# Attention and channel mix in one hand-ordered slot pipeline, heads in pairs, LayerNorm scale at the final add

## Chip, core and metric

The kernel runs on one core of one Trainium2 chip. The metric is the device time of one execution in microseconds (us), the median of several runs; lower is better. Below, PE is the matrix engine (TensorE; its weight loads are PEld), DVE the vector engine, ACT the scalar engine, POOL the GpSimd engine and SP the engine that only issues DMAs.

## What is computed

The reference is a decayed linear attention followed by a channel mix with LayerNorm and a residual. B, H, S, D are 4, 8, 768, 48; the model width is C = 384 and the hidden width F = 1536.

```python
def _attn_ref(r, k, v, w, u):
    for t in range(S):
        kt, vt, rt = (k[:, :, t].copy(), v[:, :, t].copy(), r[:, :, t].copy())
        cur = np.einsum('bhd,bhe->bhde', u[None] * kt, vt)
        y[:, :, t] = np.einsum('bhd,bhde->bhe', rt, state + cur)
        state = w[None, :, :, None] * state + np.einsum('bhd,bhe->bhde', kt, vt)
...
def _moe_ref(x, g_ln, w_ch1, w_ch2):
    xn = (x - mu) / np.sqrt(var + 1e-06) * g_ln
    ch = np.maximum(xn @ w_ch1, 0.0) @ w_ch2
    return (x + ch).astype(np.float32)
```

All inputs and the output are float32; the kernel computes its products in bf16 and sums them in float32.

## The kernel before

Time is cut into 24 tiles of 128 tokens (4 batches of 6). The kernel has two stages, and the instruction order on each engine inside a stage is chosen by the framework's scheduler from the dependencies; nothing is ordered by hand.

Set-up (lines 96 to 208): a table of powers of the decay is built on DVE by doubling (`_powers2`, lines 19 to 52), transposed on PE (lines 144 and 152) and copied into `F2`, the factors by which r and k are scaled.

Attention (lines 287 to 418), for each tile: POOL issues three DMAs that convert r, k and v to bf16 (lines 295, 299, 303; r and k have 4 buffers). DVE scales r and k (`sc`, line 308) and forms the current-token term (`uk`, `rk`, `cc8`, `Vb`, lines 312 to 318). Then, for two groups of four heads each: eight transposes per group (lines 331 and 337), one head at a time, a copy to `trb` on ACT (line 344), four score products (`at_ps`, line 348), a copy on ACT and a mask multiply on DVE (`Bm`, lines 356 and 357), and products of 48 columns for the output and the state (lines 372, 380, 388, 396). The state is scaled on DVE (`zr`, line 404). The attention result `x_sb` (line 411) stays on chip for all 24 tiles.

Channel mix (lines 428 to 467): only after the attention has given its PSUM banks back. The tiles go in six groups of four. LayerNorm statistics and the normalised `xn` come from DVE and ACT (lines 240 to 253), three transposes per tile from PE (line 267), each copied on ACT with the LayerNorm gain (line 270). `hps` (line 441) multiplies by w1 with 512 columns at a time, the ReLU goes to DVE and ACT in turn (lines 449 and 451), `ops` (line 456) multiplies by w2 with 384 columns, and DVE adds the residual (`ot`, line 464) before SP stores it (line 467). The two weights are loaded by POOL with a cast (lines 220 and 221).

Of the kernel before, what the change touches and what calls it, by code (L numbers as in the profile page):

```python
# [12 lines left out]
AX = mybir.AxisListType  # L13

MM_DT = BF16
AT_DT = BF16


def _powers2(nc, tilefn, seed_w, D, H, ncols1, ncols2):
    PW = tilefn([D, H, ncols1], FP32, name="PW2")  # L20
    PI = tilefn([D, H, ncols2], FP32, name="PI2")
    nc.vector.memset(PW[:, :, 0:1], 1.0)
    nc.vector.memset(PI[:, :, 0:1], 1.0)
    seed_w(PW[:, :, 1])
    nc.vector.reciprocal(out=PI[:, :, 1:2], in_=PW[:, :, 1:2])
    n1 = 2
    n2 = 2
    while n1 < ncols1 or n2 < ncols2:
        for T, n, ncols in ((PW, n1, ncols1), (PI, n2, ncols2)):
            if n >= ncols:  # L30
                continue
            nc.vector.tensor_tensor(
                out=T[:, :, n : n + 1],
                in0=T[:, :, n - 1 : n],
                in1=T[:, :, 1:2],
                op=ALU.mult,
            )
        for T, n, ncols in ((PW, n1, ncols1), (PI, n2, ncols2)):
            if n >= ncols:
                continue  # L40
            hi = min(2 * n, ncols)
            cnt = hi - (n + 1)
            if cnt > 0:
                nc.vector.tensor_tensor(
                    out=T[:, :, n + 1 : hi],
                    in0=T[:, :, 1 : 1 + cnt],
                    in1=T[:, :, n : n + 1].to_broadcast([D, H, cnt]),
                    op=ALU.mult,
                )
        n1 = min(2 * n1, ncols1)  # L50
        n2 = min(2 * n2, ncols2)
    return PW, PI
# [3 lines left out]
def kernel(  # L56
# [23 lines left out]
    NTT = B * NCH  # L80
    TG = 4
    NG = NTT // TG

    assert D <= DP
    assert H % 2 == 0 and S % L == 0
    assert C % P == 0 and F % P == 0
    assert NTT % TG == 0
# [33 lines left out]
    if AT_DT == FP32:  # L121
        mask_at = mask_f
    else:
        mask_at = const.tile([P, P], AT_DT, name="mask_at")
        nc.vector.tensor_copy(mask_at[:], mask_f[:])

    PW2, PI2 = _powers2(
        nc,
        const.tile,
        lambda col: nc.sync.dma_start(out=col, in_=w.rearrange("h d -> d h")),  # L130
        D,
        H,
        2 * L,
        2 * L + 1,
    )

    PWtokP = const.tile([P, H, DP], AT_DT, name="PWtokP")
    INVtokP = const.tile([P, H, DP], AT_DT, name="INVtokP")
    nc.vector.memset(PWtokP[:, :, D:DP], 0.0)
    nc.vector.memset(INVtokP[:, :, D:DP], 0.0)  # L140
    with tc.tile_pool(name="ps_setup", bufs=1, space=bass.MemoryType.PSUM) as ps_setup:
        pw_ps = ps_setup.tile([P, H, D], FP32, name="pw_ps")
        for hh in range(H):
            nc.tensor.transpose(
                out=pw_ps[:, hh, :],
                in_=PW2[:, hh, L : 2 * L],
                identity=ident_f[:D, :D],
            )
        nc.scalar.copy(out=PWtokP[:, :, :D], in_=pw_ps[:])
        iv_ps = ps_setup.tile([P, H, D], FP32, name="iv_ps")  # L150
        for hh in range(H):
            nc.tensor.transpose(
                out=iv_ps[:, hh, :],
                in_=PI2[:, hh, L + 1 : 2 * L + 1],
                identity=ident_f[:D, :D],
            )
        nc.scalar.copy(out=INVtokP[:, :, :D], in_=iv_ps[:])

    F2 = const.tile([P, 2, H, DP], AT_DT, name="F2")
    nc.vector.tensor_copy(out=F2[:, 0, :, :], in_=PWtokP[:])  # L160
    nc.vector.tensor_copy(out=F2[:, 1, :, :], in_=INVtokP[:])

    WLq = const.tile([D, H, D], FP32, name="WLq")
    nc.vector.tensor_copy(out=WLq[:], in_=PW2[:, :, L : L + 1].to_broadcast([D, H, D]))

    U_f = const.tile([P, H, D], FP32, name="U_f")
    nc.sync.dma_start(
        out=U_f[:],
        in_=bass.AP(tensor=u.tensor, offset=u.offset, ap=[[0, P], *u.ap]),
    )  # L170
    U_b = const.tile([P, H, D], AT_DT, name="U_b")
# [12 lines left out]
    rk_bufs = []
    for i in range(NSTG):
        rkt = const.tile([P, 2, H, DP], AT_DT, name=f"rk_st{i}")
        nc.gpsimd.memset(rkt[:, :, :, D:DP], 0.0)
        rk_bufs.append(rkt)

    HG = 4  # L190
    NHG = H // HG
    assert H % HG == 0
    NTRB = 4
    trb = []
    for i in range(NTRB):
        t_ = const.tile([P, 2 * HG, P], AT_DT, name=f"trb{i}")
        nc.vector.memset(t_[:], 0.0)
        trb.append(t_)
    trb_ctr = [0]

    zr = []
    for g_ in range(NHG):
        group_slots = []
        for i in range(2):
            z_ = const.tile([P, HG, D], AT_DT, name=f"zr{g_}_{i}")
            nc.vector.memset(z_[:], 0.0)
            group_slots.append(z_)
        zr.append(group_slots)
# [289 lines left out]
```

## Time and profile before

| | us |
|---|---|
| median of 3 runs | 233.95 |
| lowest, highest run | 232.15, 234.10 |
| span of the profiled execution, first to last instruction | 232.1 |
| PE busy, DVE busy, ACT busy, POOL busy in the span | 188.6, 163.9, 121.3, 67.0 |

The profile describes one execution. Its span leaves out what lies around the first and the last instruction; no time of that execution beyond its span is given, and the runs lie between 0.05 and 2.0 us above the span. Busy times are unions of the recorded instructions of an engine. Matrix products are pipelined, so a record of a product is longer than the distance to the next one, and PE's cost is read from that distance. "Granted clock" is the share of full TensorE clock that the chip allowed: 1.00 is 2.4 GHz and 0.50 is 1.2 GHz, a value between them is a mixture of the two over a stretch.

### The profile page before, as it was taken

The page shows a single profiled execution, that of the slowest core. Times are in us where ns is not written, and L with a number is a line of the kernel's source. Part 1 is how long each engine was busy: PE and PEld are TensorE (multiplying, and loading weights), DVE is VectorE, ACT ScalarE, POOL GpSimd, SP SyncE. Part 2 cuts the span into 40 slices and gives each one's busy share as a digit, 9 for nine tenths or more (in the row PEclk, how much of TensorE's full clock was granted, in tenths as well). Part 3 has the DMA queues.
Part 4 walks back from the last instruction along what each step waited for, and adds up shares of the span by engine and source line. Part 5 has one row for each costly group of instructions (what it writes and reads, how often), then busy time and mean ns, then how long its engine had stood idle before and what let it go on. Part 6 is the DMA issues. An engine that isn't in the chain of part 4 may idle for free.

```text
span 232.1 us, 4707 instructions
## 1 busy us (share of the span) xinstructions
PE 188.6 (81%) x1799; PEld 119.2 (51%) x1808; DVE 163.9 (71%) x437; ACT 121.3 (52%) x232; POOL 67.0 (29%) x86
## 2 busy tenths in 40 slices
PE   0059657959778778696767999999999999999993
PEld 0048546748556556475543445445455455455451
DVE  4998798796998999989998895742733534343431
ACT  2018955667668697766768851831732722621310
POOL 9955644656556676741000000000000000000000
PEclk9999875695998999979955899999999999999999
DMA  5999999799999999993000002102002002002012
GB/s 53 109 127 186 123 188 103 40 72 66 58 82 86 65 78 80 69 89 17 3 1 3 0 0 103 37 0 102 34 3 102 34 30 101 7 34 103 3 55 80
DMA packets 81255, 14.66 MB, mean 63 GB/s; under 512 B 76113, under 2 KB 80849, under 8 KB 81233
## 3 DMA queue, kind: packets, MB, share of 16 engines
q0 software_dynamic: 76832, 9.44, 66.8%
q1 hardware_dynamic: 4400, 4.92, 6.2%
q8 instruction: 14, 0.23, 0.4%
q14 instruction: 9, 0.07, 0.1%
HBM read 19.07 MB, written 4.72 MB: 103 GB/s over the span
## 4 chain that ended last, share of the span: by engine, by line
PE 60%; DVE 18%; ACT 8%; issue 7%; DMA 4%; POOL 1%; SPq 0%; ACTq 0%; POOLq 0%; DVEq 0%
PE ops L456 20%; PE hps L441 20%; PE tr_ps L331 5%; PE at_ps L348 4%; PE tr_ps L337 4%; ACT trb L344 4%; DVE sc L308 3%; PE tp L267 3%; DVE x_sb L411 2%; DVE Vb L318 2%; ACT xnT_all L270 2%; DMA rk_st<-in_r_dram 2%; DVE Bm L357 1%; ACT Bm L356 1%; DMA U_f<-in_u_dram 1%
## 5 line engine op out<-in xcount | busy, mean ns | idle before, releaser
L344 ACT COPY trb<-tr_ps 48x1024 bf16<-48x1024 bf16 x48 | 46.6, 1004 | 26.7 <-PE tr_ps L337 26.6
L441 PE MATMUL hps<-xnT_all,w_sb 128*128 128x512 bf16 x207 | 56.6, 388 | 0.5 <-DVE hT L449 0.2
L456 PE MATMUL ops<-w_sb,hT 128*128 128x384 bf16 x288 | 51.8, 326 | 0.0
L449 DVE TENSOR_SCALAR hT<-hps 128x512 bf16<-128x512 f32 x36 | 24.8, 689 | 21.9 <-PE hps L441 21.5
L456 PEld LDWEIGHTS <-hT 128*128 128x128 bf16 x288 | 27.6, 98 | 22.3 <-ACT hT L451 1.5
L270 ACT ACTIVATE xnT_all<-tp,g_sb 128x128 bf16<-128x128 bf16 x72 | 23.3, 368 | 26.8 <-PE tp L267 26.1
L451 ACT ACTIVATE hT<-hps 128x512 bf16<-128x512 f32 x36 | 21.5, 597 | 28.6 <-PE hps L441 28.5
L441 PEld LDWEIGHTS <-w_sb 128*128 128x128 bf16 x216 | 20.7, 99 | 25.4 <-issue 8.1
L464 DVE TENSOR_TENSOR ot<-ops,x_sb 128x384 f32<-128x384 f32 x24 | 13.4, 557 | 28.3 <-PE ops L456 28.3
L356 ACT CAST Bm<-at_ps 128x512 bf16<-128x512 f32 x48 | 28.0, 583 | 5.2 <-PE at_ps L348 4.6
L331 PE MATMUL tr_ps<-ident_mm,sc 128*48 128x128 bf16 x192 | 23.9, 251 | 5.9 <-DVE sc L308 5.9
L348 PE MATMUL at_ps<-trb 128*128 128x128 bf16 x192 | 22.4, 250 | 7.5 <-ACT trb L344 6.9
L303 POOL DMA_DIRECT2D v_st<-in_v_dram x24 | 21.3, 889 | 22.1 <-PE y_all L380 15.1
L372 PE MATMUL y_all<-v_st,Bm 128*128 128x48 bf16 x192 | 16.9, 192 | 11.3 <-DVE Bm L357 11.2
L295 POOL DMA_DIRECT2D rk_st<-in_r_dram x24 | 21.5, 895 | 9.6 <-DVE rk L314 4.6
L337 PE MATMUL tr_ps<-ident_mm,sc 128*48 128x128 bf16 x192 | 24.2, 251 | 0.0
L357 DVE TENSOR_TENSOR Bm<-Bm,mask_at 128x512 bf16<-128x512 bf16 x48 | 19.7, 419 | 5.5 <-ACT Bm L356 4.4
L299 POOL DMA_DIRECT2D rk_st<-in_k_dram x24 | 21.3, 890 | 6.7 <-DVE uk L312 4.1
L372 PEld LDWEIGHTS <-Bm 128*128 128x128 bf16 x192 | 11.8, 99 | 16.8 <-DVE Bm L357 14.8
L348 PEld LDWEIGHTS <-trb 128*128 128x128 bf16 x192 | 12.8, 109 | 13.3 <-ACT trb L344 11.6
L331 PEld LDWEIGHTS <-sc 128*48 128x48 bf16 x192 | 14.0, 116 | 9.5 <-DVE sc L308 7.5
L267 PE MATMUL tp<-ident_mm,xn 128*128 128x128 bf16 x72 | 15.8, 233 | 2.4 <-ACT xnT_all L270 1.4
(57 smaller groups left out, 245.7 us busy)
## 6 DMA issues: line engine op xcount, KB each, us to landing
out_dram<-ot SPq DMA_DIRECT2D x24, 192.0 KB, 1.9
rk_st<-in_r_dram POOLq DMA_DIRECT2D x24, 96.0 KB, 3.9
rk_st<-in_k_dram POOLq DMA_DIRECT2D x24, 96.0 KB, 4.0
v_st<-in_v_dram POOLq DMA_DIRECT2D x24, 96.0 KB, 3.7
w_sb<-in_moe_w_ch_dram POOLq DMA_DIRECT2D x2, 1152.0 KB, 9.9
U_f<-in_u_dram SPq DMA_DIRECT2D x1, 192.0 KB, 3.1
PW<-in_w_dram SPq DMA_DIRECT2D x1, 1.5 KB, 2.1
g_sb<-in_moe_g_ln_dram SPq DMA_DIRECT2D x1, 1.5 KB, 2.8
```

Of the source, the lines that this page charges most:

```text
L267: nc.tensor.transpose(out=tp[:], in_=xn[:, kc * P : (kc + 1) * P], identity=ident_mm[:])
L270: nc.scalar.activation(out=xnT_all[:, kc, tt_ln * P : (tt_ln + 1) * P], in_=tp[:], func=ACT.Copy, scale=g_sb[:, kc : kc + 1],)
L331: nc.tensor.transpose(out=tr_ps[:, hl, :], in_=rsc[:, h0 + hl, :D], identity=ident_at[:],)
L337: nc.tensor.transpose(out=tr_ps[:, HG + hl, :], in_=ksc[:, h0 + hl, :D], identity=ident_at[:],)
L344: nc.scalar.copy(out=tr_sb[:D, :, :], in_=tr_ps[:])
L348: nc.tensor.matmul(out=at_ps[:, hl, :], lhsT=tr_sb[:, HG + hl, :], rhs=tr_sb[:, hl, :], start=True, stop=True,)
L356: nc.scalar.copy(out=Bm[:], in_=at_ps[:])
L357: nc.vector.tensor_tensor(out=Bm[:], in0=Bm[:], in1=mask_at[:].unsqueeze(1).to_broadcast([P, HG, P]), op=ALU.mult,)
L372: nc.tensor.matmul(out=y_all[:, hh, :], lhsT=Bm[:, hl, :], rhs=vs[:, hh, :], start=True, stop=(c == 0),)
L441: nc.tensor.matmul(out=hps[:], lhsT=w1_sb[:, kc, fk * P : (fk + 1) * P], rhs=xnT[:, kc, :], start=(kc == 0), stop=(kc == CK - 1),)
L449: nc.vector.tensor_relu(hT[:, fk, :], hps[:])
L456: nc.tensor.matmul(out=ops[:], lhsT=hT[:, fk, ti * P : (ti + 1) * P], rhs=w2_sb[:, fk, :], start=(fk == 0), stop=(fk == FK - 1),)
```

## The change

The body of the kernel function is written anew, and `_powers2` is gone; the lines that are removed are those of the listing above. One loop of 29 slots takes the place of the two stages, and the order on all five engines is the order in which the program is written (`manual_schedule`). In slot s the attention of tile s, the first product of the channel mix for half a group (`up`, groups of two tiles, three slots behind) and the second product for tile s-5 (`down`) are issued in alternation. So slots 0 to 2 hold attention alone, 3 and 4 attention and `up`, 5 to 23 all three, 24 to 26 `up` and `down`, and 27 and 28 `down` alone.

Other edits: two heads share one transpose of 128 columns (8 instead of 16 per tile), with one ACT copy for all; the score products read 48 rows that start at partition 0 or 64. The mask multiply reads PSUM directly (no ACT copy). The state of two heads is one 96-column block, and a zero pattern in `WLZ` removes the cross terms. The current-token term is a product with `uwI` on PE, copied by ACT (`cc`) and multiplied with v on POOL (`Vb`). The gain of the LayerNorm is multiplied into w1 once (three ACT instructions on `w1_f`, which SP loads in float32); x minus its mean goes through the products, and the reciprocal deviation is applied with the residual (`ot`). All ReLUs run on ACT. Products of `up` have 256 columns.

Not shown in the diff: the decay table `T` is one tile of 128 partitions for both signs of the exponent, doubled in 7 steps on DVE; `WLZ` and `uwI` are built after it on DVE; SP issues six small loads before those of `w1_f`; `ident` and `mask` are made on POOL after `load(0)`. Flags of products are cut.

```diff
@@ -55,413 +16,404 @@
...
+    ld = ctx.enter_context(tc.tile_pool(name="ld", bufs=8))
+    sb2 = ctx.enter_context(tc.tile_pool(name="sb2", bufs=2))
+    sb3 = ctx.enter_context(tc.tile_pool(name="sb3", bufs=3))
+    sm = ctx.enter_context(tc.tile_pool(name="sm", bufs=4))
+    xp = ctx.enter_context(tc.tile_pool(name="xp", bufs=10))
+    ps_h = ctx.enter_context(tc.tile_pool(name="ps_h", bufs=2, space=bass.MemoryType.PSUM))
+    ps = ctx.enter_context(tc.tile_pool(name="ps", bufs=1, space=bass.MemoryType.PSUM))
+    ctx.enter_context(
+        tc.manual_schedule(
+            engines={ENG.PE, ENG.DVE, ENG.Activation, ENG.Pool, ENG.SP}
+        )
+    )
...
+    def load(i):
+        b, c = divmod(i, NCH)
+        s0 = c * L
+        rk = ld.tile([P, 2, H, D], BF16, name="rk")
+        vv = ld.tile([P, H, D], BF16, name="vv")
+        nc.gpsimd.dma_start(out=rk[:, 1], in_=k[b, :, s0 : s0 + L, :].rearrange("h t d -> t h d"))
+        nc.gpsimd.dma_start(out=rk[:, 0], in_=r[b, :, s0 : s0 + L, :].rearrange("h t d -> t h d"))
+        nc.gpsimd.dma_start(out=vv[:], in_=v[b, :, s0 : s0 + L, :].rearrange("h t d -> t h d"))
+        rk_t[i], v_t[i] = rk, vv
...
+    load(0)
...
+    w1_f = const.tile([P, CK, F], FP32, name="w1_f")
+    w1_src = moe_w_ch1.rearrange("(kc p) f -> p kc f", p=P)
+    for kc in range(CK):
+        nc.sync.dma_start(out=w1_f[:, kc, :], in_=w1_src[:, kc, :])
+    w1_sb = const.tile([P, CK, F], BF16, name="w1_sb")
...
+    load(1)
+    load(2)
...
+    fps = ps.tile([P, 2, 512], FP32, name="at")
+    for kc in range(CK):
+        nc.tensor.transpose(out=fps[:, 0, kc * P : (kc + 1) * P], in_=T[:, kc, 0:L], identity=ident_f[:])
+    for kc in range(CK):
+        nc.tensor.transpose(out=fps[:, 1, kc * P : (kc + 1) * P], in_=T[:, CK + kc, 1 : L + 1], identity=ident_f[:])
+    F2 = const.tile([P, 2, H, D], BF16, name="F2")
+    nc.scalar.copy(out=F2[:], in_=fps[:, :, :C].rearrange("p a (h d) -> p a h d", h=H))
...
+    for kc in range(CK):
+        nc.scalar.activation(
+            out=w1_sb[:, kc, :], in_=w1_f[:, kc, :], func=ACT.Copy, scale=g_sb[:, kc : kc + 1]
+        )
...
+    def scale(i):
+        nc.vector.tensor_tensor(
+            out=sc_bufs[i % NSC][:, :, :, :D], in0=rk_t[i][:], in1=F2[:], op=ALU.mult
+        )
+    def transposes(i):
+        sc = sc_bufs[i % NSC].rearrange("p a (q e) d -> p (a q) (e d)", e=2)
+        tp = ps.tile([P, 2 * HP, P], BF16, name="tr")
+        for j in range(2 * HP):
+            nc.tensor.transpose(out=tp[:, j, :], in_=sc[:, j, :], identity=ident[:])
+        tr = sb3.tile([P, 2, HP, P], BF16, name="trs")
+        nc.scalar.copy(out=tr[:], in_=tp[:].rearrange("p (a q) t -> p a q t", a=2))
+        q = sb2.tile([P, HP, P], BF16, name="q")
+        nc.vector.tensor_tensor(out=q[:], in0=tr[:, 0], in1=tr[:, 1], op=ALU.mult)
+        tr_t[i] = tr
+        st[i] = q
+    def scores(i):
+        b, c = divmod(i, NCH)
+        tr, q = tr_t[i], st[i]
+        at = ps.tile([P, 2, HP, P], FP32, name="at")
+        for p in range(HP):
+            for par in range(2):
+                p0 = par * DP
+                nc.tensor.matmul(
+                    out=at[:, par, p, :],
+                    lhsT=tr[p0 : p0 + D, 1, p, :],
+                    rhs=tr[p0 : p0 + D, 0, p, :],
...
+                )
+        s_ps = ps.tile([P, 512], FP32, name="s")
+        ksc = sc_bufs[i % NSC].rearrange("p a (q e) d -> p a q (e d)", e=2)
+        first = True
+        if c < NCH - 1:
+            if c > 0:
+                nc.tensor.matmul(
+                    out=s_ps[:, : HP * E2],
+                    lhsT=ident[:],
+                    rhs=Z_t[i - 1][:].rearrange("p q e -> p (q e)"),
...
+                )
+                first = False
+            for p in range(HP):
+                nc.tensor.matmul(
+                    out=s_ps[:, p * E2 : (p + 1) * E2],
+                    lhsT=ksc[:, 1, p, :],
+                    rhs=v_t[i][:, 2 * p : 2 * p + 2, :],
...
+                )
+                first = False
+        for p in range(HP):
+            nc.tensor.matmul(
+                out=s_ps[:, C + 2 * p : C + 2 * p + 2],
+                lhsT=q[:, p, :],
+                rhs=uwI[:, p, :],
...
+            )
+            first = False
+        A = sb2.tile([P, 2, HP, P], BF16, name="A")
+        for par in range(2):
+            nc.vector.tensor_tensor(
+                out=A[:, par],
+                in0=at[:, par],
+                in1=mask[:].unsqueeze(1).to_broadcast([P, HP, P]),
+                op=ALU.mult,
+            )
+        cc = sb2.tile([P, H], FP32, name="cc")
+        nc.scalar.copy(out=cc[:], in_=s_ps[:, C : C + H])
+        Vb = sb2.tile([P, H, D], BF16, name="Vb")
+        nc.gpsimd.tensor_tensor(
+            out=Vb[:], in0=v_t[i][:], in1=cc[:].unsqueeze(2).to_broadcast([P, H, D]), op=ALU.mult
+        )
+        if c < NCH - 1:
+            Z = sb3.tile([P, HP, E2], BF16, name="Z")
+            nc.vector.tensor_tensor(
+                out=Z[:],
+                in0=s_ps[:, : HP * E2].rearrange("p (q e) -> p q e", q=HP),
+                in1=WLZ[:],
+                op=ALU.mult,
+            )
+            Z_t[i] = Z
+        A_t[i] = A
+        cc_t[i] = Vb
+    def values(i):
+        b, c = divmod(i, NCH)
+        y = ps.tile([P, 512], FP32, name="y")
+        first = True
+        if c > 0:
+            for p in range(HP):
+                nc.tensor.matmul(
+                    out=y[:, p * E2 : (p + 1) * E2],
+                    lhsT=tr_t[i][:, 0, p, :],
+                    rhs=Z_t[i - 1][:, p, :],
...
+                )
+                first = False
+        for par in range(2):
+            for p in range(HP):
+                h = 2 * p + par
+                nc.tensor.matmul(
+                    out=y[:, h * D : (h + 1) * D],
+                    lhsT=A_t[i][:, par, p, :],
+                    rhs=v_t[i][:, h, :],
...
+                )
+                first = False
+        x = xp.tile([P, C], FP32, name="x")
+        nc.vector.tensor_tensor(
+            out=x[:], in0=y[:, :C], in1=cc_t[i][:].rearrange("p h d -> p (h d)"), op=ALU.add
+        )
+        stats = sm.tile([P, nc.vector.BN_STATS_DIM], FP32, name="stats")
+        nc.vector.bn_stats(out=stats[:], in_=x[:])
+        if i % GT == 0:
+            mv_t[i // GT] = sm.tile([P, GT, nc.vector.BN_AGGR_DIM], FP32, name="mv", bufs=6)
+        mv = mv_t[i // GT]
+        nc.vector.bn_aggr(out=mv[:, i % GT, :], in_=stats[:])
+        xn = sb3.tile([P, C], BF16, name="xn")
+        nc.vector.tensor_scalar(
+            out=xn[:], in0=x[:], scalar1=mv[:, i % GT, 0:1], scalar2=None, op0=ALU.subtract
+        )
+        x_t[i], xn_t[i] = x, xn
+        if i % GT == GT - 1:
+            rs = sm.tile([P, GT], FP32, name="rs", bufs=6)
+            nc.scalar.activation(out=rs[:], in_=mv[:, :, 1], func=ACT.Sqrt, bias=eps_t[:], scale=1.0)
+            nc.vector.reciprocal(out=rs[:], in_=rs[:])
+            mv_t[i // GT] = rs
...
+    def ln_transposes(i):
+        g, j = divmod(i, GT)
+        if j == 0:
+            xT_t[g] = sb3.tile([P, CK, GW], BF16, name="xT")
+        tp = ps.tile([P, 2 * HP, P], BF16, name="tr")
+        for kc in range(CK):
+            nc.tensor.transpose(out=tp[:, kc, :], in_=xn_t[i][:, kc * P : (kc + 1) * P], identity=ident[:])
+        nc.scalar.copy(out=xT_t[g][:, :, j * P : (j + 1) * P], in_=tp[:, :CK, :])
+    def up(g, m):
+        if m == 0:
+            hT_t[g] = sb2.tile([P, FK, GW], BF16, name="hT")
+        hp = ps_h.tile([P, 2, GW], FP32, name="hp")
+        for f in range(2):
+            fk = 2 * m + f
+            for kc in range(CK):
+                nc.tensor.matmul(
+                    out=hp[:, f, :],
+                    lhsT=w1_sb[:, kc, fk * P : (fk + 1) * P],
+                    rhs=xT_t[g][:, kc, :],
...
+                )
+        nc.scalar.activation(out=hT_t[g][:, 2 * m : 2 * m + 2, :], in_=hp[:], func=ACT.Relu)
+    NM = 3
+    PM = FK // NM
+    def down(i, m):
+        g, j = divmod(i, GT)
+        if m == 0:
+            o_t[i] = ps.tile([P, 512], FP32, name="o")
+        o = o_t[i]
+        for fk in range(m * PM, (m + 1) * PM):
+            nc.tensor.matmul(
+                out=o[:, :C],
+                lhsT=hT_t[g][:, fk, j * P : (j + 1) * P],
+                rhs=w2_sb[:, fk, :],
...
+            )
+        if m == NM - 1:
+            ot = sb3.tile([P, C], FP32, name="ot")
+            nc.vector.scalar_tensor_tensor(
+                out=ot[:],
+                in0=o[:, :C],
+                scalar=mv_t[g][:, j : j + 1],
+                in1=x_t[i][:],
+                op0=ALU.mult,
+                op1=ALU.add,
+            )
+            b, c = divmod(i, NCH)
+            nc.sync.dma_start(out=out[b, c * L : (c + 1) * L, :], in_=ot[:])
...
+    UP0 = 3
+    DN0 = 5
+    NB = FK // 2
+    def up_slot(s, n_):
+        q_ = s - UP0
+        if q_ < 0:
             return
+        g, j = divmod(q_, GT)
+        if g < NT // GT:
+            up(g, j * (NB // GT) + n_)
+    def down_slot(s, n_):
+        i_ = s - DN0
+        if 0 <= i_ < NT:
+            down(i_, n_)
+    scale(0)
+    for s in range(NT + DN0):
+        att = s < NT
+        if att:
+            transposes(s)
+        if s + 3 < NT and s + 3 not in rk_t:
+            load(s + 3)
+        if s == 0:
             nc.gpsimd.dma_start(out=w2_sb[:], in_=w2_src)
+        up_slot(s, 0)
+        down_slot(s, 0)
+        if att:
+            scores(s)
+            if s + 1 < NT:
+                scale(s + 1)
+        up_slot(s, 1)
+        if 0 <= s - 1 < NT:
+            ln_transposes(s - 1)
+        down_slot(s, 1)
+        if att:
+            values(s)
+        up_slot(s, 2)
+        down_slot(s, 2)
```

## Rows read from the trace of the kernel before

**Rows 1.** The page's chain of work that ended last, share of the span by engine.

```profile
PE 60%; DVE 18%; ACT 8%; issue 7%; DMA 4%; POOL 1%; SPq 0%; ACTq 0%; POOLq 0%; DVEq 0%
```

**Rows 2.** Windows: stretch and its length, busy us (instructions) per engine, clock, DMA, GB/s.

```profile
30.00:46.00 16.00, 12.07 (x157) 9.56 (x153) 13.53 (x38) 8.66 (x14) 8.75 (x10) 0.65 1.38 106
58.00:70.00 12.00, 9.10 (x156) 7.05 (x153) 11.86 (x31) 7.80 (x11) 7.05 (x9) 0.93 1.30 70
...
137.70:232.10 94.40, 89.91 (x503) 46.87 (x507) 41.56 (x83) 33.07 (x85) 0.00 (x0) 1.00 0.14 51
```

**Rows 3.** Chain in order of time, 150 to 163 us: start, us, work (PE at full clock).

```profile
153.47 1.29 PE hps L441 x6
154.76 6.88 PE ops L456 x42
161.64 0.11 PE tp L267 x2
```

**Rows 4.** Timeline of PE at full clock: start, us; first and last of 8 in alternation.

```profile
82.33 0.19 PE L388 MATMUL s_ps<-v_st,sc 128*48 128x48 bf16 x1
...
82.50 0.18 PE L396 MATMUL s_ps<-zr,ident_mm 128*48 128x48 bf16 x1
```

**Rows 5.** Groups by line, ACT: busy us, mean ns of one | idle before.

```profile
L344 ACT COPY trb<-tr_ps 48x1024 bf16<-48x1024 bf16 x48 | 46.6, 1004 | 26.7 <-PE tr_ps L337 26.6
L451 ACT ACTIVATE hT<-hps 128x512 bf16<-128x512 f32 x36 | 21.5, 597 | 28.6 <-PE hps L441 28.5
L157 ACT CAST INVtokP<-iv_ps 128x384 bf16<-128x384 f32 x1 | 0.5, 478 | 0.9 <-PE iv_ps L152 0.9
L244 ACT ACTIVATE rstd<-mv,eps_t 128x1 f32<-128x1 f32 x24 | 6.6, 291 | 1.6 <-DVE mv L242 1.5
```

**Rows 6.** Groups by line, DVE.

```profile
L449 DVE TENSOR_SCALAR hT<-hps 128x512 bf16<-128x512 f32 x36 | 24.8, 689 | 21.9 <-PE hps L441 21.5 <-PE tp L267 0.5
L357 DVE TENSOR_TENSOR Bm<-Bm,mask_at 128x512 bf16<-128x512 bf16 x48 | 19.7, 419 | 5.5 <-ACT Bm L356 4.4
L308 DVE TENSOR_TENSOR sc<-rk_st,F 128x1024 bf16<-128x1024 bf16 x24 | 16.2, 678 | 0.0
L411 DVE TENSOR_TENSOR x_sb<-y_all,Vb 128x384 f32<-128x384 f32 x24 | 13.2, 552 | 0.9 <-PE y_all L380 0.8
L318 DVE TENSOR_TENSOR Vb<-v_st,cc 128x384 bf16<-128x384 bf16 x24 | 13.1, 544 | 0.0
L240 DVE BATCH_NORM_STATS2 stats<-x_sb 128x6 f32<-128x384 f32 x24 | 12.5, 536 | 0.0
L253 DVE TENSOR_SCALAR xn<-x_sb,mv,rstd 128x384 bf16<-128x384 f32 x24 | 11.7, 487 | 1.4 <-PE tp L267 1.2
L242 DVE BATCH_NORM_AGGREGATE mv<-stats 128x2 f32<-128x6 f32 x24 | 3.6, 165 | 0.0
```

**Rows 7.** Timeline of DVE: two instructions that don't wait for each other.

```profile
118.10 0.52 DVE L240 BATCH_NORM_STATS2 stats<-x_sb 128x6 f32<-128x384 f32 x1
118.55 0.53 DVE L318 TENSOR_TENSOR Vb<-v_st,cc 128x384 bf16<-128x384 bf16 x1
```

**Rows 8.** Groups by line, POOL: a DMA issue and an elementwise instruction.

```profile
L303 POOL DMA_DIRECT2D v_st<-in_v_dram x24 | 21.3, 889 | 22.1 <-PE y_all L380 15.1 <-PE y_all L372 6.0 <-DVE Vb L318 0.9
masks.py:199 POOL TENSOR_SCALAR_AFFINE_SELECT ident_f<-ident_f 128x128 f32<-128x128 f32 x1 | 0.3, 287 | 0.0
```

**Rows 9.** The page's DMA issues: KB each as written, median us from issue to landing.

```profile
rk_st<-in_r_dram POOLq DMA_DIRECT2D x24, 96.0 KB, 3.9
w_sb<-in_moe_w_ch_dram POOLq DMA_DIRECT2D x2, 1152.0 KB, 9.9
```

**Rows 10.** Chain in order of time: end of the power table, first transposes, last instruction.

```profile
11.14 1.13 DVE PI L44
...
16.14 0.62 PE tr_ps L331 x4
...
228.39 0.56 DVE ot L464
```

More of the change, by code (lines that the diff above doesn't have):

```diff
@@ L12 @@
 ACT = mybir.ActivationFunctionType
[L13 to L52, printed above, removed]
+ENG = mybir.EngineType
 @with_exitstack
@@ L79 @@
     FK = F // P
[L80 to L87, printed above, removed]
+    GT = 2
+    GW = GT * P
+    E2 = 2 * D
+    assert D <= DP and H % 2 == 0 and S % L == 0 and C % P == 0 and F % P == 0
     assert tuple(out.shape) == (B, S, C)
     const = ctx.enter_context(tc.tile_pool(name="const", bufs=1))
-    xpool = ctx.enter_context(tc.tile_pool(name="xpool", bufs=1))
-    x_sb = xpool.tile([P, NTT, C], FP32, name="x_sb")
@@ L120 @@
     )
[L121 to L171, printed above, removed]
@@ L184 @@
[L184 to L208, printed above, removed]
@@ L263, in emit_ln_transposes @@
-    def emit_ln_transposes(tt_ln, ps_tp):
-        xn = xn_tiles.pop(tt_ln)
-        for kc in range(CK):
-            tp = ps_tp.tile([P, P], MM_DT, name="tp")
-            nc.tensor.transpose(
-                out=tp[:], in_=xn[:, kc * P : (kc + 1) * P], identity=ident_mm[:]
-            )
-            nc.scalar.activation(
-                out=xnT_all[:, kc, tt_ln * P : (tt_ln + 1) * P],
-                in_=tp[:],
-                func=ACT.Copy,
-                scale=g_sb[:, kc : kc + 1],
-            )
@@ new lines @@
+    T = const.tile([P, 2 * CK, L + 1], FP32, name="T")
+    nc.vector.memset(T[:, :, 0:1], 1.0)
+    nc.vector.tensor_copy(T[:, 0:CK, 1], w_c[:])
+    nc.vector.reciprocal(out=T[:, CK : 2 * CK, 1], in_=w_c[:])
+    n = 1
+    while n < L:
+        nc.vector.tensor_tensor(
+            out=T[:, :, n + 1 : 2 * n + 1],
+            in0=T[:, :, 1 : n + 1],
+            in1=T[:, :, n : n + 1].to_broadcast([P, 2 * CK, n]),
+            op=ALU.mult,
+        )
+        n *= 2
+    fps = ps.tile([P, 2, 512], FP32, name="at")
@@ new lines @@
+    n = 2
+    while n < L:
+        nc.vector.tensor_tensor(out=wl[:], in0=wl[:], in1=wl[:], op=ALU.mult)
+        n *= 2
+    assert n == L
+    WLZ = const.tile([P, HP, E2], FP32, name="WLZ")
+    nc.vector.memset(WLZ[:], 0.0)
+    uwI = const.tile([P, HP, 2], BF16, name="uwI")
+    nc.vector.memset(uwI[:], 0.0)
+    for par in range(2):
+        p0 = par * DP
+        nc.vector.tensor_copy(
+            out=WLZ[p0 : p0 + D, :, par * D : (par + 1) * D],
+            in_=wl[p0 : p0 + D, :].unsqueeze(2).to_broadcast([D, HP, D]),
+        )
+        nc.vector.tensor_tensor(
+            out=uwI[p0 : p0 + D, :, par], in0=u_p[p0 : p0 + D, :], in1=w_p[p0 : p0 + D, :], op=ALU.mult
+        )
@@ new lines @@
+    NSC = 3
+    sc_bufs = []
+    for i in range(NSC):
+        t_ = const.tile([P, 2, H, DP], BF16, name=f"sc{i}")
+        nc.vector.memset(t_[:, :, :, D:DP], 0.0)
+        sc_bufs.append(t_)
+    for kc in range(CK):
+        nc.scalar.activation(
+            out=w1_sb[:, kc, :], in_=w1_f[:, kc, :], func=ACT.Copy, scale=g_sb[:, kc : kc + 1]
+        )
+    tr_t, cc_t, Z_t, A_t, x_t, mv_t, xn_t, st = {}, {}, {}, {}, {}, {}, {}, {}
+    def scale(i):
+        nc.vector.tensor_tensor(
+            out=sc_bufs[i % NSC][:, :, :, :D], in0=rk_t[i][:], in1=F2[:], op=ALU.mult
+        )
```

308 lines of the change are left out of this document (58 added, 250 removed).

## The prediction, made before the change was run

> **What bounds the kernel now.** I read the chain of work first, then the windows, then the distances between products on PE, and last the costs by line. The chain lies on PE for 60% of the span and on DVE for 18% [rows 1], but that share is a mean over two stages with different limits. In the channel mix from 137.7 us on, PE is busy 89.9 of 94.4 us at full clock while DVE is busy 41.6 and ACT 33.1 [rows 2]: PE bounds it and the other engines stand half empty. In the attention it is the reverse: between 58 and 70 us DVE is busy 11.86 of 12 us and PE 9.1; between 30 and 46 us DVE has 13.5 of 16 us and the granted clock is 0.65 [rows 2]. Attention begins at 16.1 us [rows 10] and the channel mix needs all of it, so a tile pays for DVE first and for PE afterwards. Whatever lets the two stages share time can win up to the smaller of the two.
>
> **PE per slot, all at full clock.** A 512-column product costs 1.29/6 = 0.215 us and a 384-column one 6.88/42 = 0.164; two transposes of 128 columns, with 128-column weights, take 0.11, so 0.056 each [rows 3]. Small products start (82.50-82.33)/7 = 0.025 us apart [rows 4]. A full slot has 18 products of 256 columns (half of 0.215: 1.94 us), 12 of 384 (1.97), 8 pair transposes, 8 scores and 3 LayerNorm transposes of 128 (19 x 0.056 = 1.06), 8 of 48 columns (0.20), 8 of 96 (96/384 of 0.164, 0.33), one of 384 (0.16) and 4 of two columns (0.10): 5.8 us. A tile of before needs on the same prices 3.91 + 27 x 0.056 + 32 x 0.025 = 6.2. So the pairing itself saves only 0.4 us a tile on PE; the rest must come from overlap.
>
> The Trainium skill, page "TensorE: Matmul & The Clock Gate", section "Back-to-back issue gap", speaks against the 0.056: it gives about 81 ns per product in a sustained stream of 128-column products with their weight loads. By it 19 products would cost 0.5 us more per slot and the kernel some 9 us more. The row of this kernel, of the same shapes, shows 0.056, and I go by that.
>
> **DVE per slot.** `A` reads PSUM twice with 512 elements, as the ReLU of line 449 does: 2 x 0.69. `q` is as line 357: 0.42. `scale` has 768 elements between the 512 of line 357 (0.42) and the 1024 of line 308 (0.68): 0.55. `Z` and `x` are as line 411 (0.55 each), statistics 0.54, aggregate 0.17, `xn` 0.49, and `ot` again as line 411, 0.55 [rows 6]. Sum 5.2 us. Instructions that don't wait for each other start 0.45 apart where one lasts 0.52 [rows 7], so up to 0.07 each comes back. Gone from DVE are line 312 to 318's work and half of the ReLUs. **ACT**: one 1024-element copy 1.0 (before: two), three ReLUs 0.6 each, one 384-element copy 0.48, a small copy and half a square root, near 0.29 for one [rows 5]: 3.7 us, no bound. **POOL**: three DMA issues at 0.89 (2.7 us) [rows 8] and `Vb`. No row shows a two-input product on POOL. From below I take line 318's 0.54 on DVE [rows 6]; from above three times the 128-element instruction of POOL, 0.86, and twice that, 1.7, for the second input [rows 8]. I take the middle, 1.1.
>
> **The walk through a full slot.** Order on PE: transposes, `up`, `down`, scores, state and `cc`, `up`, LayerNorm transposes, `down`, values, `up`, `down`. Take the start of the scores as 0. The scores take 0.45; results are readable some 0.2 us after a product starts [rows 4], so DVE gets `A` at 0.6, and with 0.07 of overlap each it does A, A, Z and the next `scale` until 2.8. Values on PE end after 0.45 + 0.43 + 0.65 + 0.17 + 0.66 + 0.37 = 2.7, readable at 2.9: `x` 2.95 to 3.5, statistics to 4.1, aggregate to 4.3, `xn` to 4.8, `ot` to 5.3. The buffer of `down` has one copy, so the next `down` on PE may start only at 5.3; without that wait it would be there at 5.2. It takes 0.66, then come the next scores: 6.0 us. In every second slot ACT's queue holds the square root behind the aggregate (4.3 to 4.6), then the last ReLU (to 5.2), then the copy of the next transposes (to 6.1), and the scores wait for that: 6.1. So three loops, PE alone at 5.8, DVE with `ot` at 6.0, ACT in odd slots at 6.1, lie almost on each other; I take 6.1. Both ends: 5.8, if nothing waits, and 7.2, if `Vb` is late or DVE's instructions stretch. `cc` is ready at about 1.3 and `x` wants `Vb` at 2.95, so `Vb` is free up to 1.6 us; past that each 0.1 us costs 0.1 us per slot, 19 times. Queued behind `Vb` on POOL are the loads of the tile three slots on; they land in 3.9 us [rows 9], with two slots, 12 us, to cover them, and a slot asks for three loads in 6.1 us where POOL of before issued nine in 12 us, a tile in 4.0 [rows 2]. The stores on SP have a slot each to cover them.
>
> **The start.** The first scaling no longer waits for the long power chain, whose last step ended at 12.3 us [rows 10]. But ACT's queue has, ahead of the first copy of transposes, the three scalings of w1: 1536 elements at 1.0 us per 1024 [rows 5] is 1.5 each. ACT can't begin them before the table copy, which I put at 9.5 us (an estimate from the 12.3, since the longest step now has 384 elements and not 1016), so they end at 14 at the earliest; and they wait for `w1_f`. The two loads of the weights of before, each 2304 KB of float32 in HBM and 1152 KB written, took 9.9 us [rows 9]; w1 is issued on SP behind six small loads, each at most the 0.89 of POOL [rows 8], so between 1 and 6 us; at 3.5 it lands at 13.4 by what is read or at 23 by what is written, plus 1.5. I take ACT free at 16.5 (nearer the first, since nothing else is large), bounds 14 and 25. The first scores start 1.1 later, at 17.6. Slots 0 to 2 are a latency chain: scores to `A` 0.6, `A`, `Z`, `scale` 2.2, transposes 0.7, copy 1.0, waits 0.3, so 4.8 at full clock. PE is mostly idle there and I expect half clock, as little denser attention was granted 0.65 [rows 2]: the 0.45 of transposes and of scores double, 5.4 each. Slots 3 and 4 have 3.8 us of PE at full clock, 7.7 at half; 12.5 for the two while the clock comes up (9.8 to 17).
>
> **The sum.** First scores 17.6; slots 0 to 2, 16.2; 3 and 4, 12.5; 19 full slots of 6.1, 115.9; that is the place of the scores in slot 24, 1.8 us after its start, so minus 1.8. Slots 24 to 26: 3.9 us of PE and 0.2 of waiting for `ot`: 12.3. Slots 27 and 28: 1.97 and a wait of 0.8 for `ot`, since no `up` covers it: 5.6. After the last product 0.55 for `ot` and the store: the end came 3.7 us after `ot` began in before (232.1 - 228.39) [rows 10], so 3.7. Together 182 us of span against 232.1. Runs lay 0 to 2 us above the span of before, the median 1.9; I predict 183.
>
> **The rivals.** One: *POOL and DVE in each other's way.* `Vb` is the first arithmetic on POOL in the loop, and it falls where DVE does `A`, `Z` and `scale`. If DVE stands still for its 1.1 us in each slot, or `Vb` takes 2.7 us, the loop is 7.2 us: 203. For it: DVE is already the tightest loop. Against it: DVE of before was busy 11.86 of 12 us beside nine issues on POOL [rows 2]. The Trainium skill, "GPSIMD Engine Reference", section "Engine selection", advises VectorE for elementwise work and calls GpSimd about two times slower with two inputs; its "Key points" say that the two share SBUF interfaces, above all when a DVE instruction has two SBUF inputs. Of the DVE work here that is `q` and `scale`. By twice line 318 `Vb` takes 1.1 us (an estimate from that page), and no run here shows it yet.
>
> Two: *better than the walk.* w1 lands early, ACT is free at 14, the clock is full from slot 3, and PE's 5.8 is the slot: 15.1 + 14.4 + 9.8 + 110.2 - 1.8 + 12 + 5.2 + 3.7 = 169.
>
> Three, on the other side: *PE stays at 1.2 GHz.* The granted clock fell to 0.65 where PE had 12.1 busy of 16 us. If the waits in a slot bring that on, a slot needs 11.6 us of PE, and the sum is 182 + 19 x 5.5 = 286, slower. It decides from 182 + 19 x (slot - 6.1) = 232, a slot of 8.7 us, a mean clock of 0.67. Against it: PE is wanted for 5.8 of 6.1 us, as dense as the stretch that had 1.00 [rows 2].
>
> Four: *the overlap doesn't come.* In-order queues might line the two stages up one behind the other inside each slot: 4.0 us of attention per tile (nine loads in 12 us) to 5.1 ((137.7-16.1)/24, the whole stage and the way into the next), and 94.4/24 = 3.9 of channel mix [rows 2, 10], 7.9 to 9.0 us; at 8.7 nothing has changed, 232. For it: every PSUM tile but `hp` has one buffer. Against it: the walk finds two products of another stage between each producer and its consumer.
>
> **How the numbers follow.** Forecast (174 to 192): 0.60. Rival one (192 to 215): 0.21. Rival two (166 to 174): 0.10. Rival three: 0.05. Rival four: 0.04. The likeliest has its own range, 174 to 192. The range for 8 in 10 reaches from 170, half of rival two, to 206, most of rival one. One per cent, 2.3 us, is about what a measurement here can tell from no change: faster 0.92 (forecast, one, two and some of four), same 0.02, slower 0.06.
>
> **What would show it.** Right: `ot` at a distance of 6.0 to 6.2 us in slots 5 to 23, PE busy over 90% at a granted clock of 1.00 there, DVE between 4.5 and 5.3 us per slot, `down`'s first product waiting for `ot` and scores for ACT in odd slots; `Vb` under 1.6 us and never what `x` waits for; the first transposes' copy right behind the third scaling of w1, near 16.5. Wrong: a clock under 0.9 in the full slots, `x` waiting for POOL, DVE instructions longer than their rows, an ACT queue that holds the transposes' copy in even slots too, or w1 landing past 20 us.

## The result and the profile after

The changed kernel takes 182.68 us (median; 182.46 to 183.27) against 233.69 us: a ratio of 0.785, with a 95% interval from 0.781 to 0.790. Its profiled execution has a span of 181.2 us. The page's busy times and chain of the changed kernel:

```profile
PE 148.7 (82%) x1646; PEld 110.1 (61%) x1646; DVE 125.7 (69%) x278; ACT 87.3 (48%) x162; POOL 85.9 (47%) x105
...
PE 47%; DVE 33%; issue 8%; DMA 5%; ACT 4%; SPq 2%; DVEq 0%
```

The windows by stage (columns as in [rows 2]): start, attention alone, the way in, the full slots from the scores of slot 5 to those of slot 23, and the two stretches of the end.

```profile
0.00:17.00 17.00, 3.16 (x24) 2.33 (x25) 6.35 (x32) 7.71 (x6) 12.83 (x21) 1.00 1.40 190
17.00:34.00 17.00, 11.99 (x139) 9.26 (x139) 14.80 (x31) 6.76 (x13) 10.90 (x14) 1.00 1.77 139
34.00:46.00 12.00, 10.28 (x121) 7.97 (x119) 8.91 (x21) 7.07 (x15) 7.62 (x10) 0.86 1.05 55
...
44.10:154.90 110.80, 104.90 (x1237) 78.11 (x1238) 90.65 (x187) 59.34 (x118) 54.64 (x63) 1.00 0.88 73
...
160.00:172.00 12.00, 11.53 (x87) 8.23 (x86) 1.56 (x3) 5.15 (x9) 0.00 (x0) 1.00 0.14 50
172.00:181.20 9.20, 4.22 (x24) 2.24 (x23) 1.53 (x3) 0.00 (x0) 0.00 (x0) 1.00 0.19 66
```

In the full slots PE is busy 95% and DVE 82% of one and the same stretch, where before one was full in one stage and the other in the other [rows 2]. What PE and ACT still wait for in 45 to 158 us (waits: who, for whom, us in total, times, longest):

```profile
ACT rs L314 <- DVE mv L306: 15.2, 9, 1.7
...
PE o L355 <- DVE ot L364: 5.7, 16, 0.5
...
ACT trs L190 <- PE tr L188: 4.5, 9, 0.5
PEld L203 <- ACT trs L190: 2.9, 9, 0.3
```

The timeline of PE gives the slots: the eight score products of slots 0, 1, 2, 3, 4 and 5, and of slot 23 (start, us for all eight).

```profile
16.39 0.61 PE L203 MATMUL at<-trs 48*128 48x128 bf16 x8 [4.16 <-ACT trs L190]
21.52 0.61 PE L203 MATMUL at<-trs 48*128 48x128 bf16 x8 [1.10 <-ACT trs L190]
27.06 0.61 PE L203 MATMUL at<-trs 48*128 48x128 bf16 x8 [1.47 <-ACT trs L190]
32.33 0.40 PE L203 MATMUL at<-trs 48*128 48x128 bf16 x8
38.04 0.40 PE L203 MATMUL at<-trs 48*128 48x128 bf16 x8 [1.72 <-ACT trs L190]
44.12 0.40 PE L203 MATMUL at<-trs 48*128 48x128 bf16 x8
...
154.76 0.40 PE L203 MATMUL at<-trs 48*128 48x128 bf16 x8
```

From slot 5 to 23 it is (154.76 - 44.12)/18 = 6.15 us a slot. That is a mean of unlike slots, as the scores of slots 9 to 13 show; tile 11 is the last of its batch and tile 12 the first of the next:

```profile
68.67 0.40 PE L203 MATMUL at<-trs 48*128 48x128 bf16 x8
74.95 0.40 PE L203 MATMUL at<-trs 48*128 48x128 bf16 x8
81.19 0.40 PE L203 MATMUL at<-trs 48*128 48x128 bf16 x8
87.16 0.40 PE L203 MATMUL at<-trs 48*128 48x128 bf16 x8
93.23 0.40 PE L203 MATMUL at<-trs 48*128 48x128 bf16 x8
```

The slot of an inner tile, one with a neighbour of its batch on either side, takes 6.28 us (odd slots) or 6.24 (even ones), the last tile's 5.97 and the first tile's 6.07.

### The profile page after: what moved, and what is told of

It is laid out like the page before. It is cut to its first block, busy times and chain, and to the rows that moved or that the text cites. A ratio compares the mean times of both kernels' runs of the same rounds, so it can differ in the third digit from the quotient of the medians.

```text
span 181.2 us, 4089 instructions
## 1 busy us (share of the span) xinstructions
PE 148.7 (82%) x1646; PEld 110.1 (61%) x1646; DVE 125.7 (69%) x278; ACT 87.3 (48%) x162; POOL 85.9 (47%) x105
## 4 chain that ended last, share of the span: by engine, by line
PE 47%; DVE 33%; issue 8%; DMA 5%; ACT 4%; SPq 2%; DVEq 0%
PE o L355 20%; PE hp L337 11%; DVE ot L364 8%; DVE stats L302 7%; DVE x L298 7%; DMA w_f<-in_moe_w_ch_dram 5%; PE at L203 5%; DVE xn L308 3%; DVE A L246 3%; DVE mv L306 2%; DVE Z L260 2%; ACT trs L190 2%; PE y L288 2%; PE s L215 2%; PE tr L327 2%
## 5 line engine op out<-in xcount | busy, mean ns | idle before, releaser
L355 PE MATMUL o<-w_sb,hT 128*128 128x384 bf16 x288 | 57.8, 325 | 8.0 <-DVE ot L364 7.7
L337 PE MATMUL hp<-xT,w_sb 128*128 128x256 bf16 x432 | 60.5, 277 | 0.0
L344 ACT ACTIVATE hT<-hp 128x512 bf16<-128x512 f32 x72 | 42.8, 597 | 25.4 <-PE hp L337 25.4
L255 POOL TENSOR_TENSOR Vb<-vv,cc 128x384 bf16<-128x384 bf16 x24 | 19.8, 826 | 66.5 <-ACT cc L253 66.5
L337 PEld LDWEIGHTS <-w_sb 128*128 128x128 bf16 x432 | 38.8, 99 | 5.1
L246 DVE TENSOR_TENSOR A<-at,mask 128x512 bf16<-128x512 f32 x48 | 30.9, 685 | 9.5 <-PE at L203 9.2
L190 ACT COPY trs<-tr 128x1024 bf16<-128x1024 bf16 x24 | 24.2, 1006 | 9.1 <-PE tr L188 9.1
L71 POOL DMA_DIRECT2D rk<-in_k_dram x24 | 22.6, 944 | 0.8 <-POOLq L432 0.8
L72 POOL DMA_DIRECT2D rk<-in_r_dram x24 | 21.3, 889 | 3.0 <-DMA vv<-in_v_dram 3.0
L73 POOL DMA_DIRECT2D vv<-in_v_dram x24 | 21.8, 907 | 0.0
L188 PE MATMUL tr<-ident,sc 128*128 128x128 bf16 x192 | 16.5, 236 | 4.1 <-DVE sc L180 4.1
L203 PEld LDWEIGHTS <-trs 48*128 48x128 bf16 x192 | 5.8, 98 | 15.9 <-ACT trs L190 13.1
L180 DVE TENSOR_TENSOR sc<-rk,F 128x768 bf16<-128x768 bf16 x24 | 13.4, 558 | 0.0
```

Source lines behind the costliest of these rows:

```text
L71: nc.gpsimd.dma_start(out=rk[:, 1], in_=k[b, :, s0 : s0 + L, :].rearrange("h t d -> t h d"))
L73: nc.gpsimd.dma_start(out=vv[:], in_=v[b, :, s0 : s0 + L, :].rearrange("h t d -> t h d"))
L188: nc.tensor.transpose(out=tp[:, j, :], in_=sc[:, j, :], identity=ident[:])
L190: nc.scalar.copy(out=tr[:], in_=tp[:].rearrange("p (a q) t -> p a q t", a=2))
L203: nc.tensor.matmul(out=at[:, par, p, :], lhsT=tr[p0 : p0 + D, 1, p, :], rhs=tr[p0 : p0 + D, 0, p, :], start=True, stop=True,)
L246: nc.vector.tensor_tensor(out=A[:, par], in0=at[:, par], in1=mask[:].unsqueeze(1).to_broadcast([P, HP, P]), op=ALU.mult,)
```

## The experiments

**The overlap undone.** The loop over slots is split; buffers of what lies between the stages are enlarged.

```diff
-    for s in range(NT + DN0):
...
+    for s in range(NT):
+        transposes(s); load(s + 3); scores(s); scale(s + 1); ln_transposes(s - 1); values(s)
+    for s in range(UP0, NT + DN0):
+        up_slot(s, 0); down_slot(s, 0); up_slot(s, 1); down_slot(s, 1); up_slot(s, 2); down_slot(s, 2)
```

> The same instructions as the changed kernel, but first the attention of all 24 tiles, then `up` and `down` of all: the overlap is undone, the pairing and the other edits stay. Theory (all of the gain is overlap): first scores at 16.4, 24 slots of 5.0 to 5.4, then 22 slots of 4.1 and the ends: 235 to 250 us, no faster than the kernel before. Rival (pairing, the direct mask and the product for the current token bring half or more): under 210.

Measured 251.17 us, ratio to the kernel before 1.081 (1.075 to 1.087). The rewritten operations alone, in this hand order but in two stages, are slower than the old kernel by 8%: none of the gain shows without the interleaving, which is worth 68 us to them. Two things were not tried: the old operations interleaved, and the rewritten ones in two stages with an order and buffers made for that (`down` still has one buffer here). Its windows, attention and channel mix:

```profile
17.00:145.00 128.00, 80.65 (x914) 61.40 (x913) 103.93 (x222) 42.84 (x85) 73.74 (x85) 1.00 1.00 59
150.00:240.00 90.00, 88.53 (x653) 63.54 (x651) 13.27 (x22) 39.14 (x66) 0.00 (x0) 1.00 0.13 47
```

Now no engine is full in the attention: it is the chain of one tile, 5.1 to 5.6 us, as in slots 0 to 2 of the changed kernel.

**PE filled in the two-stage version.**

```diff
         transposes(s)
+        dummy(5)
...
+        dummy(4)
         values(s)
+        dummy(3)
```

> The two-stage version with 12 products of 384 columns added per attention tile on PE, whose result nobody reads, in the places where PE waits for the copy of the transposes, for the mask and for the next scaling. Theory (in the two-stage version PE's products run at half rate because PE is mostly idle, and the dense channel mix of the changed kernel lifts that): transposes and scores take 0.6 us less per tile, 251 less 12 to 18, about 236, with more work. Rival (rate is not what costs; the chain does): same, or slower by up to the added 2 us per tile.

Measured 238.72 us, ratio 1.030 (1.026 to 1.034): 12.5 us faster with 288 products more. The timelines of PE, transposes of one tile, first in the two-stage version and then with PE filled:

```profile
82.81 1.03 PE L188 MATMUL tr<-ident,sc 128*128 128x128 bf16 x8 [0.59 <-DVE sc L180]
```

```profile
82.88 0.62 PE L188 MATMUL tr<-ident,sc 128*128 128x128 bf16 x8 [0.17 <-DVE sc L180]
```

In these two traces the transposes start 0.107 us apart in the first and 0.056 in the second, and 0.056 is what one takes at full clock [rows 3]: the sparse attention ran at 1.2 GHz, the filled one at 2.4. So of the 68 us of interleaving at least 12.5 come from PE's rate and not from work done side by side; at least, since the added products may cost time of their own.

**What sets the slot: `ot`, the square root, or PE.** Three runs. In the first, `xn` and the reciprocal follow `ot` on DVE; in the second only the square root and the reciprocal follow the last `down`; the third does both.

```diff
-        xn = sb3.tile(...)          # in values(i)
...
         down_slot(s, 2)
+        if att:
+            center(s)               # xn, then (third run: square root and) reciprocal
```

> On DVE the last multiply-add of a tile (`ot`) is written ahead of `xn`; the square root stays on ACT, the reciprocal goes behind `xn`. Theory one (the single buffer of `down` makes PE wait for `ot`: 7.7 us in the waits of the changed kernel): `ot` comes 0.6 us earlier, PE's wait for it vanishes, but in odd slots the square root still delays the copy of the transposes, some 0.35 us each; 4 to 5 us faster, about 178. Rival (PE's 5.8 us and ACT's queue set the slot, `ot` only happens to end last): within 1 us of 182.7.

> The changed kernel with only the square root and the reciprocal moved behind the last `down` of the slot, so that on ACT they no longer stand ahead of the last ReLU and the copy of the transposes. Theory (PE waits for `ot` in all slots, odd ones too): at most 1 us faster, about 182. Rival (ACT's queue sets the odd slots): 3 us faster.

> Both moves together: `ot` ahead of `xn`, and the square root behind the last `down`. Theory (once `ot` is out of the way, ACT's queue is what PE waits for in odd slots, 0.2 to 0.3 us each, and nothing else): 175.1 less 2 to 3, about 172.5, slots of 5.8 us in odd and even ones. Rival (PE's own 5.8 us already bounds the version with `ot` first): 175.

| | us | ratio (95%) |
|---|---|---|
| `ot` first | 175.11 | 0.753 (0.749 to 0.757) |
| square root late | 181.00 | 0.780 (0.777 to 0.783) |
| both | 172.51 | 0.745 (0.741 to 0.749) |

`ot` first gives 7.6 us, more than the 4 to 5 expected, and by the profiles 6.5 of them lie between the scores of slot 5 and those of slot 23 (104.15 us for 110.64); `xn`, now behind it, is also shorter (mean 435 ns for 586, next experiment). The square root alone gives 1.7 us by the medians, but its interval overlaps that of the changed kernel, and between the same scores it is only 0.5 us (110.11 for 110.64); PE still waits for `ot` 18 times there; in both versions with `ot` first it no longer does in the full slots. With `ot` first, the square root is worth the 2.6 us that were expected. Scores of three slots in a row, with `ot` first (an even distance, then an odd and an even one), then with both:

```profile
83.52 0.40 PE L203 MATMUL at<-trs 48*128 48x128 bf16 x8 [0.19 <-ACT trs L190]
...
88.95 0.40 PE L203 MATMUL at<-trs 48*128 48x128 bf16 x8
94.98 0.40 PE L203 MATMUL at<-trs 48*128 48x128 bf16 x8 [0.19 <-ACT trs L190]
100.75 0.40 PE L203 MATMUL at<-trs 48*128 48x128 bf16 x8
```

```profile
93.31 0.40 PE L203 MATMUL at<-trs 48*128 48x128 bf16 x8
99.08 0.40 PE L203 MATMUL at<-trs 48*128 48x128 bf16 x8
...
44.50:148.00 103.50, 103.50 (x1254) 79.38 (x1253) 85.94 (x188) 61.63 (x120) 54.61 (x63) 1.00 0.95 79
```

With `ot` first the slots of inner tiles are 6.03 (odd) and 5.77 us (even) in turn; the 5.43 is the slot of a batch's first tile, which has no products with an earlier state. With both, odd and even ones are 5.77, those of a batch's first and last tile 5.44 (the last forms no new state), the mean from slot 5 to 23 is 5.66, and the window shows PE busy 103.5 of 103.5 us. That is PE's own bound, 5.8 in the prediction, which gave every tile the work of an inner one.

**POOL's loads.** `if s + 3 < 8: load(s + 3)`, else the tiles of eight slots earlier are used again.

> The changed kernel, but only tiles 0 to 7 are loaded and later tiles reuse their r, k and v: what is left out is 48 of the 72 loads. Theory (POOL's issuing of the loads stretches `xn` on DVE from 0.42 to 0.6 us and more, and `xn` lies in the loop that sets the slot): `xn` at 0.42 in all slots from 5 on, 0.2 us per slot for some 16 slots, 3 us faster. Rival (the stretch is hidden, or it comes from `Vb`): within 1 us.

Measured 178.93 us, ratio 0.773 (0.769 to 0.777), 2.8 us less by the ratios ((0.785 - 0.773) x 233). The durations of `xn` (ns, least/median/most), changed kernel and then without the later loads:

```profile
L308 DVE TENSOR_SCALAR xn<-x,mv x24: 419/619/843, 20.6 to 158.7; 128x384 bf16<-128x384 f32 x24
```

```profile
L308 DVE TENSOR_SCALAR xn<-x,mv x24: 419/420/837, 21.5 to 156.2; 128x384 bf16<-128x384 f32 x24
```

The scores of slots 13, 14 and 15 without the later loads are 6.11 and 6.03 us apart, where they are 6.28 and 6.24 in slots 9 to 11 of the changed kernel:

```profile
92.17 0.40 PE L203 MATMUL at<-trs 48*128 48x128 bf16 x8
98.28 0.40 PE L203 MATMUL at<-trs 48*128 48x128 bf16 x8
104.31 0.40 PE L203 MATMUL at<-trs 48*128 48x128 bf16 x8
```

This run takes away the transfers together with their issuing. The timelines of POOL and DVE tell the two apart. First a stretched `xn` of the changed kernel, then one of the two-stage version beside the same issue:

```profile
66.27 0.90 POOL L73 DMA_DIRECT2D vv<-in_v_dram  x1
66.72 0.63 DVE L308 TENSOR_SCALAR xn<-x,mv 128x384 bf16<-128x384 f32 x1
```

```profile
83.93 1.03 POOL L73 DMA_DIRECT2D vv<-in_v_dram  x1
84.07 0.42 DVE L308 TENSOR_SCALAR xn<-x,mv 128x384 bf16<-128x384 f32 x1
```

In these two traces every `xn` that starts 0.25 to 0.46 us after an issue began ends 0.18 us after that issue does. Those that start in its first 0.14 us, or from 0.67 us on, take 0.42 us. So it is the issuing that stretches `xn`, and only where it falls badly.

`Vb` disturbs DVE too, but not in the full slots. There it ends before `scale` begins or overlaps it by 0.1 us, and `scale` takes 0.55 us. Where the two run side by side, in two slots of the changed kernel (1 and 2) and in most tiles of the two-stage version, `scale` takes 0.65 to 0.71 us, also when no loads are left to issue, as here in the two-stage version:

```profile
124.11 0.83 POOL L255 TENSOR_TENSOR Vb<-vv,cc 128x384 bf16<-128x384 bf16 x1 [2.12 <-ACT cc L253]
124.64 0.71 DVE L180 TENSOR_TENSOR sc<-rk,F 128x768 bf16<-128x768 bf16 x1
```

**`Vb` on DVE.** The POOL instruction becomes one of DVE behind `Z`.

> `Vb` moves from POOL to DVE, behind `Z`. Theory (POOL's 0.83 us lies free beside DVE and `x` waits 0.2 us for PE): DVE does A, A, Z, Vb and scale before `x`, 0.47 us more than there is room for by 0.2 to 0.3; about 5 us slower, 187 to 189. Rival (POOL's arithmetic and DVE are in each other's way): same or faster.

Measured 186.20 us, ratio 0.803 (0.797 to 0.809): 3.5 us slower. On POOL `Vb` takes 826 ns and on DVE 547; the slower engine is the right place, since no wait of the changed kernel names `Vb` as what `x` waits for. `A` and `Z` last as long with `Vb` on DVE as with it on POOL (686 and 547 ns for 685 and 547).

**The scalings of w1 later.**

```diff
-    for kc in range(CK):
-        nc.scalar.activation(out=w1_sb[:, kc, :], ...)
...
             scores(s)
+            if s < CK:
+                scale_w1(s)
```

> The three scalings of w1 on ACT go into slots 0, 1 and 2, behind the small copy of `cc`. Theory (they hold the first copy of transposes, which was ready for 12.3 and ran at 15.3): first scores at 13.4 instead of 16.4, 3 us faster, about 179.7. Rival (the loads of tiles 1 to 3, or the clock, would then hold slots 0 to 2 longer): less than 1 us.

Measured 181.13 us, ratio 0.779 (0.774 to 0.784). The first scores did come at 13.34 instead of 16.39, but half of it was given back, and the interval of the ratio overlaps that of the changed kernel. The timeline of ACT in slot 1 of this version shows where:

```profile
20.89 1.58 ACT L172 ACTIVATE w_sb<-w_f,g_sb 128x1536 bf16<-128x1536 f32 x1
22.37 0.47 ACT L328 COPY xT<-tr 128x384 bf16<-128x384 bf16 x1
22.86 1.28 ACT L314 ACT_TABLE_LOAD   x1
24.15 0.30 ACT L314 ACTIVATE rs<-mv,eps_t 128x2 f32<-128x2 f32 x1
24.35 0.99 ACT L190 COPY trs<-tr 128x1024 bf16<-128x1024 bf16 x1
```

The scaling, the LayerNorm copy and the first load of the square root's table (1.28 us) stand ahead of the next copy of transposes, and slot 1 lasts 6.66 us (18.74 to 25.40) instead of 5.54.

**All moves together.** The moves of the third `ot` run, and the scalings of w1 behind the LayerNorm copy, loads behind `Vb`, one early square root for the table, and a second bank at the end:

```diff
-            o_t[i] = ps.tile([P, 512], FP32, name="o")
+            o_t[i] = ps.tile([P, 512], FP32, name="y" if i >= NT - DN0 and i % 2 else "o")
```

> All the moves that the runs so far point to: `ot` ahead of `xn`, square root behind the last `down`; the scalings of w1 in slots 0 to 2 behind the LayerNorm copy; the loads of a slot behind `Vb` in POOL's queue; the table of the square root loaded before the first copy; and in slots 24 to 28 the bank of `y` as a second buffer of `down`. Theory (slot, start and end are independent terms): 172.5 for the slot, less 3 for the start, less 2.3 for the end, 167. Rival (a later start of the loads, or ACT in slots 0 to 2, takes the start's part back): 170 or more.

Measured 167.47 us, ratio 0.724 (0.720 to 0.728): faster than both kernels, and by the sum of the parts. Its windows, way in, full slots and end:

```profile
13.50:40.00 26.50, 19.49 (x240) 15.02 (x238) 21.97 (x48) 16.05 (x26) 18.44 (x21) 1.00 1.61 113
40.00:145.00 105.00, 105.00 (x1276) 80.62 (x1276) 87.20 (x191) 62.31 (x122) 58.37 (x68) 1.00 1.03 83
145.00:165.30 20.30, 16.39 (x121) 11.45 (x119) 4.71 (x10) 6.60 (x12) 0.00 (x0) 0.96 0.17 59
```

PE has no idle time in the full slots by these records; what is left to win there is PE's own stream of products.

## Why the prediction was right, point by point

| term | forecast | measured |
|---|---|---|
| first scores | 17.6 | 16.4 |
| slots 0 to 2 | 16.2 | 32.33 - 16.39 = 15.9 |
| slots 3 and 4 | 12.5 | 44.12 - 32.33 = 11.8 |
| one full slot | 6.1 | 6.15 |
| span | 182 | 181.2 |
| median | 183 | 182.7 |

The last `ot` starts at 177.31, so the tail is 3.9 us for 3.7.

**The walk.** The loop that was named does set the slot: the next `down` waits for `ot`, 16 times in the full slots for 5.7 us. It runs through PE as well, since `x` waits for the values, which come behind two blocks of channel mix; that is the walk's 2.95 us. The second loop, ACT in odd slots, was real and in second place, as the pair of runs on it shows: beside `ot` it adds 0.04 us to an odd slot (6.28 against 6.24), with `ot` out of the way 0.26 (6.03 against 5.77).

The mechanism was right, but that the mean came so close is partly luck, since two errors cancel. Slots of inner tiles take 6.24 and 6.28 us, not 6.0 and 6.1, because the loads stretch `xn`; with the later loads left out they take 6.03 and 6.11, which are the walk's own numbers. And the prediction counted 19 slots with the work of an inner tile, while every sixth tile reads no earlier state and every sixth forms no new one; their slots, 6.07 and 5.97, pull the mean down again. "DVE instructions longer than their rows" was a sign of being wrong, and it did show, on one instruction.

**The durations.** `A` 685 ns, `scale` 558, `Z` 547, `x` 554 and `q` 425 are within 3% of the rows taken for them [rows 6]. Two were undersized: `ot` 602 for 0.55, and `xn` 586 for 0.49 (0.62 to 0.79 us in the full slots up to slot 19, 0.42 behind them); the issuing of loads on POOL is the cause for `xn`. `Vb` was oversized, 0.83 for 1.1. The 128-column transposes cost 0.056 to 0.06 us here too (eight in 0.61 with the run-out of the last), so the page "TensorE: Matmul & The Clock Gate" of the Trainium skill, "Back-to-back issue gap", with its 81 ns, does not hold for this kernel.

**The start.** The last part of w1 landed at 13.84 us, 13.4 expected, and the copy of the transposes followed the third scaling at 15.34, 16.5 expected. The step was right; its worth was tested by moving it. Slots 3 and 4 came out near the forecast with a stretch at 1.2 GHz inside them (granted clock 0.50 from 39.1 to 42.4 us), which no other profile of this loop has; there the two take 9.8 to 11.5 us.

**The rivals.** POOL and DVE do disturb each other, but the later loads cost 2.8 us, not the 21 of that rival; `Vb` itself is free in the full slots, and moving it to DVE costs 3.5. The "Key points" of the Trainium skill's "GPSIMD Engine Reference" name two kinds of DVE instruction that contend with GpSimd, those in a 2-port perf mode and those with two SBUF inputs; the prediction kept the second and looked at `q` and `scale`. The trace agrees for `scale`, 0.70 us beside `Vb` for 0.55; no run shows in which mode `xn` works. The advice of the Trainium skill, "GPSIMD Engine Reference", "Engine selection", against elementwise work on GpSimd would have cost those 3.5 us here; its factor of two for two inputs was 826/547 = 1.5. Better than the walk: the slot that PE alone sets exists (5.66 us in the mean), but two moves away. PE at 1.2 GHz: in the full slots the distances are those of full clock; but the mechanism that the rival feared is what the two-stage version shows. No overlap: the two-stage version, where the stages share no time, took 251 us, more than the 216 to 237 that the prediction gave that rival. The estimate took 4.0 to 5.1 us of attention and 3.9 of channel mix per tile, from before; in two stages the new attention takes 5.1 to 5.6, with PE at half rate, and a slot of the channel mix 4.13 (its `down` starts at 153.66 and 157.79 us), 0.22 of it waiting for `ot`.

## What to carry to other kernels

Two stages that fill different engines can be worth interleaving even where the rewritten operations alone are slower. Then walk one slot by hand along the single-buffered tiles: the loop that closes through them (here `down`, `ot`, `down`) sets the slot. Moving an instruction that nobody waits for yet (`xn`) out of it was worth 7.6 us, and making the same instruction shorter in its place 2.8. Count the work of every kind of slot and not of the fullest alone. A slot's order should keep long work out of an in-order queue ahead of what the next slot needs (the square root, the scalings of w1).
